# Scaling the first expert's outputs: GpSimd for groups 0 and 1, gated ScalarE for the others, in a linear attention and mixture-of-experts kernel

## The chip, the cores and the metric

One core of a Trainium2 chip runs the whole program. The metric is the device time of one execution in microseconds, the median of several runs. A core has TensorE (PE, matmuls into PSUM), VectorE (DVE), ScalarE (ACT), GpSimd (POOL, which here reads and writes SBUF only) and SyncE (SP, used here to issue DMAs). Each engine works through its own instruction queue in order; semaphores tie the queues together.

## The reference

The first half is linear attention over 8 batches and 8 heads (576 rows each, 64 wide); its output becomes `x` of 4608 rows by 512. The second half, where the change lies, is a mixture of 8 experts in which every row goes through every expert, weighted by a table `P` that a Sinkhorn iteration balances:

```python
logits = x @ w_gate
P = np.exp(logits - logits.max())
for _ in range(8):
    P /= P.sum(1, keepdims=True) + 1e-09
    P /= P.sum(0, keepdims=True) + 1e-09
    P *= N / E
out = np.zeros((N, D), dtype=np.float32)
for e in range(E):
    h = np.maximum(x @ w1[e], 0.0)
    ye = h @ w2[e]
    out += P[:, e:e + 1] * ye
```

`w1[e]` is 512 by 1024, `w2[e]` is 1024 by 512. The term of expert 0 is `P[:, 0:1] * y0`, and the sum over experts runs in an accumulator in SBUF.

## The kernel before

**Tiling.** The 4608 rows are nine groups g of 512 rows. `acc[g]` is the float32 accumulator of a group, four tiles `ts` of 128 rows by 512. Accumulators 0 to 4 live in SBUF from the start and serve as landing buffers for attention inputs at first; 5 to 8 are allocated when the attention's buffers are released (the event "late").

**Expert 0** (lines 749 to 804, 882 to 885) runs in ordinary matmuls, partly between the attention's steps. At that time P isn't known yet, so `down0` copies its result unscaled from PSUM into `acc[g]`: tiles with even `ts` on VectorE (L802), with odd `ts` on ScalarE (L795); `up0` has its relu on ScalarE (L760). Meanwhile `routing` computes P (its last step is L945 on VectorE).

**Experts 1 to 7** (lines 1284 to 1304) use a Strassen-like scheme with seven products in place of eight. For each expert, `sums_w` makes sums of weight blocks on VectorE (L986: first four for `w1`, then four for `w2`). For each group, `up7` makes 14 up products (names x1, y1, x2, w1, x3, x4, w2, each for two halves `fp`; a product is four matmuls of 256 columns, L1078). Its helpers empty the PSUM banks: `keep` copies a bank into a buffer U on ScalarE (L1106), `add` adds U and a bank into `hT` on VectorE (L1110), `relu` writes `hT` on ScalarE (L1115). A bank that `keep` has copied takes the next product on top (x1, x2, x3, x4 in one bank), so the next product waits for the copy. `down7` makes four sums S of `hT` blocks (L986) and seven down products of eight matmuls each, X1, Y1, Z1, X2, X3, Z2, X4. `read` adds P times a bank into an accumulator on VectorE (L1218). `read2` does it in two steps: ScalarE writes P times the bank into a buffer V (L1230, there are two V), and GpSimd adds V into the accumulator (L1233). The products go through `read2` for X1 and Y1 into block (0,0) and for Z1 and X3 into block (1,1), through `read` for the others.

**Order.** The down products of group g lie between the up products of group g+1, by

```python
ORDER = "X1 x10 w10 x11 X2 x20 y10 x21 Z1 y11 X3 w11 x30 x31 x40 x41 w20 Y1 w21 X4 Z2".split()
```

so Y1 comes near the end of the next group's slot. The first group of expert 1 has expert 0's last down matmuls ahead of it, and no down products of its own scheme between its up products.

**The planner.** The order in which instructions enter each engine's queue isn't the order of the text. `Plan.op` records each operation with its engine, a duration from a model (for instance `act(el)`: el/1200 + 0.09 us; `pool(el)`: el x 1.64e-3 + 0.17 us), the keys that it reads (`r`) and writes (`w`), and a running number. A read waits for the last writer of its key so far, a write for the last writer and all readers. `schedule` then takes, again and again, the operation that can start earliest by the model, at equal start the one with the lowest number. An operation marked `shared` (all of GpSimd's, and VectorE's sums L986 and some of the routing's) also waits until the one before it that was marked `shared` is done (`self.port`). The order so found is written into the queues; on the chip only the order and the semaphores remain.

**The scaling.** For expert 1, `down7` multiplies the accumulator of its group by column 0 of P, four operations of 128x512 on ScalarE (L1240). They need P, the unscaled result of expert 0 in `("acc", g, ts)` and, for accumulators 5 to 8, `akey(g)`, which is "late". They write `("acc", g, ts, j)` for both column halves j, and the reads of the down products (L1218, L1233) add on top of that. They have no other dependency: all 36 can start as soon as P and the tile are there. The operations of the group's S sums have lower numbers than its scaling, its down products and all later groups have higher ones.

Of the kernel before, what the change touches and what calls it, by code (L numbers as in the profile page):

```python
# [12 lines left out]
ALU = mybir.AluOpType  # L13
ACT = mybir.ActivationFunctionType
# [214 lines left out]
def kernel(  # L229
# [11 lines left out]
    nc = tc.nc  # L241
# [3 lines left out]
    N, DD = out.shape  # L245
# [24 lines left out]
    P = const.tile([128, NT, E], FP32, name="P")  # L270

    NA = 5
    acc = [accp.tile([128, 4, DD], FP32, name=f"acc{g}", tag=f"acc{g}") for g in range(NA)]
# [20 lines left out]
    def act(el, fn, r=(), w=()):  # L294
        plan.op("ACT", el / 1200.0 + 0.09, 0.22, fn, r, w)

    def dve(el, fn, r=(), w=(), shared=False):
        plan.op("DVE", el / 960.0 + 0.09, 0.22, fn, r, w, shared=shared)

    def pool(el, fn, r=(), w=()):  # L300
        plan.op("POOL", el * 1.64e-3 + 0.17, 0.25, fn, r, w, shared=True)
# [49 lines left out]
    def new(tag):  # L351
        return banks.new(int(tag[1])) if tag in ("P1", "P2") else R[tag].new()
# [426 lines left out]
    def akey(g):  # L779
        return ["late"] * (g >= NA) + ["P"] * (g >= 9)  # L780
# [31 lines left out]
    for i, (queue, eng) in enumerate((("ACT", nc.scalar), ("POOL", nc.gpsimd))):  # L812
        dma(queue, 1 << 15, 100, lambda i=i, eng=eng: eng.dma_start(
            out=wphi_f[64 * i:64 * i + 64, :], in_=w_phi), w=[f"wphi_f{i}"])
# [4 lines left out]
    for i in range(2):  # L819
        dve(64, lambda i=i: nc.vector.tensor_copy(  # L820
            out=wphi2[64 * i:64 * i + 64, i, :], in_=wphi_f[64 * i:64 * i + 64, :]),
# [4 lines left out]
    for h0 in (4, 6):  # L826
# [3 lines left out]
        out=wgate, in_=moe_w_gate.rearrange("(c p) e -> p c e", p=128)), w=["wgate"])  # L830
    for i in range(2):
        for x in range(2):
            dve(300, lambda i=i, x=x: nc.vector.memset(vrd[i][x], 0.0),
                w=[("vrd", i, x, h, *y) for h in range(2) for y in ((), (1,))])
# [147 lines left out]
    def sub(eng, el, out_, x, y, op, r, w):  # L982
        f = nc.vector if eng is dve else nc.gpsimd
        kw = {"shared": True} if eng is dve else {}
        eng(el * 0.6 if eng is dve else el * 1.04 + 128,
            lambda: f.tensor_tensor(out=out_(), in0=x(), in1=y(), op=op), r, w, **kw)  # L986
# [85 lines left out]
    def product(bank, lhs, rhs, nk, r, first, takes=(), wk=()):  # L1072


        for i in range(2):
            for k in range(nk):
                z = i == 0 and k == 0
                pe(256, lambda i=i, k=k, z=z: nc.tensor.matmul(  # L1078
                    bank()[:, 256 * i:256 * i + 256], lhsT=lhs(k, i), rhs=rhs(k),
                    start=first and z, stop=k == nk - 1, skip_group_check=True),  # L1080
                    r, [bank, *(wk if z else ())], takes if z else ())
# [72 lines left out]
    def acc_part(g, i, j):  # L1154
        return lambda: acc[g][:, 2 * i:2 * i + 2, 256 * j:256 * j + 256]
# [17 lines left out]
    def down7(e, g, hT, B7):  # L1173


        def a(i, j):
            return lambda: hT[j]()[:, :, 256 * i:256 * i + 256]

        def hk(i, j):
            return [(hT[j], fp, i) for fp in range(2)]  # L1180

        late, seen = akey(g), set()
        S = [new("S") for _ in range(4)]
        S01 = dve
        sub(dve, 1024, lambda: S[2](), a(0, 0), a(1, 0), ALU.subtract, hk(0, 0) + hk(1, 0),
            [S[2]])
        sub(S01, 1024, lambda: S[0](), a(1, 0), a(1, 1), ALU.add, hk(1, 0) + hk(1, 1), [S[0]])
        sub(S01, 1024, lambda: S[1](), lambda: S[0](), a(0, 0), ALU.subtract,
            [S[0]] + hk(0, 0), [S[1]])
        sub(dve, 1024, lambda: S[3](), a(0, 1), lambda: S[1](), ALU.subtract,  # L1190
            [S[1]] + hk(0, 1), [S[3]])

        def prod(bank, lhs, y, r, first, more=()):
            f, r2 = B7[y]
            product(bank, lambda k, i: lhs()[:, k, 128 * i:128 * i + 128],
                    lambda k: f()[:, k, :], 4, r + r2 + (["P"] if e else late) + list(more), first)

        def start(bank, i, j):

            out_ = acc_part(g, i, j)  # L1200
            w = [("acc", g, 2 * i + n, j) for n in range(2)]
            if (i, j) in seen:
                dve(500, lambda: nc.vector.tensor_tensor(
                    out=out_(), in0=bank().rearrange("p (a b) -> p a b", a=2), in1=out_(),
                    op=ALU.add), [bank] + late, w)
            else:
                act(512, lambda: nc.scalar.copy(
                    out=out_(), in_=bank().rearrange("p (a b) -> p a b", a=2)),
                    [bank] + late, w)
            seen.add((i, j))  # L1210

        def read(bank, i, j):

            if e == 0:
                return start(bank, i, j)
            for n in range(2):
                ts = 2 * i + n
                dve(330, lambda n=n, ts=ts: nc.vector.scalar_tensor_tensor(  # L1218
                    out=acc[g][:, ts, 256 * j:256 * j + 256],
                    in0=bank()[:, 256 * n:256 * n + 256], scalar=P[:, 4 * g + ts, e:e + 1],  # L1220
                    in1=acc[g][:, ts, 256 * j:256 * j + 256], op0=ALU.mult, op1=ALU.add),
                    [bank, "P"], [("acc", g, ts, j)])

        def read2(bank, i, j):

            if e == 0:
                return start(bank, i, j)
            u = new("V")
            for n in range(2):
                act(390, lambda n=n: nc.scalar.activation(  # L1230
                    out=u()[:, n, :], in_=bank()[:, 256 * n:256 * n + 256], func=ACT.Copy,
                    bias=0.0, scale=P[:, 4 * g + 2 * i + n, e:e + 1]), [bank, "P"], [(u, n)])
            pool(670, lambda: nc.gpsimd.tensor_tensor(  # L1233
                out=acc[g][:, 2 * i:2 * i + 2, 256 * j:256 * j + 256],
                in0=acc[g][:, 2 * i:2 * i + 2, 256 * j:256 * j + 256], in1=u(), op=ALU.add),
                [(u, 0), (u, 1)], [("acc", g, 2 * i + n, j) for n in range(2)])

        if e == 1 and g < 9:
            for ts in range(4):
                act(512, lambda ts=ts: nc.scalar.activation(  # L1240
                    out=acc[g][:, ts, :], in_=acc[g][:, ts, :], func=ACT.Copy, bias=0.0,
                    scale=P[:, 4 * g + ts, 0:1]), ["P", ("acc", g, ts)] + akey(g),
                    [("acc", g, ts, j) for j in range(2)])
        x, y, z = new("P1"), new("P1"), new("P1")

        def X1():
            prod(x, a(0, 0), "11", hk(0, 0), True, S[1:3])
            read2(x, 0, 0)

        def Y1():  # L1250
            prod(y, a(0, 1), "21", hk(0, 1), True)
            read2(y, 0, 0)

        def Z1():
            prod(z, lambda: S[0](), "t1", [S[0]], True, S[3:4])
            read2(z, 1, 1)

        def X2():
            prod(x, lambda: S[1](), "t2", [S[1]], False)
            read(x, 0, 1)  # L1260

        def X3():
            prod(x, lambda: S[2](), "t3", [S[2]], False)
            read2(x, 1, 1)

        def Z2():
            prod(z, lambda: S[3](), "22", [S[3]], False)
            read(z, 0, 1)

        def X4():  # L1270
            prod(x, a(1, 1), "t4", hk(1, 1), False)
            read(x, 1, 0)

        def stores():
            if e == E - 1:
                for ts in range(4):
                    store(g, ts)

        return {"out": stores, "X1": X1, "Y1": Y1, "Z1": Z1, "X2": X2, "X3": X3, "Z2": Z2, "X4": X4}
# [4 lines left out]
    for e in range(1, E):  # L1284
        w1, w2 = load_w(e, ["late"])
        if e == 1:
            for g in range(NG):
                sums_x(g)
        A7, B7 = sums_w(e, w1, w2)
        for g in (range(NG) if e < E - 1 else [8, *range(8)]):  # L1290
            X = load_x(g)
            hT = [new("hT") for _ in range(2)]
            un = up7(A7, g, X, hT, ["up0"])
            for n in ORDER:
                if len(n) == 3:
                    un[n[:2], int(n[2])]()
                elif dn is not None:
                    dn[n]()
            if dn is not None:
                dn["out"]()  # L1300
            if e == E - 1 and g == 7:
                down8(e, g, hT, w2)
            else:
                dn = down7(e, g, hT, B7)
# [31 lines left out]
```

## Time and profile before

| | |
|---|---|
| median of 3 runs | 1036.67 us (1035.63 to 1037.01) |
| the profiled execution | 1036.16 us |
| its span from first to last instruction | 1034.4 us |
| granted TensorE clock | 1.000 |
| TensorE busy (matmul) | 1013.8 us, 98% of the span |
| weight loads | 843.0 us, 81% |
| VectorE busy | 823.7 us, 80% |
| ScalarE busy | 710.9 us, 69% |
| GpSimd busy | 462.8 us, 45% |

In the page's 40 slices, the busy tenths show attention and expert 0 in the first ten slices and the experts after them:

```profile
PE   7899999999999999999999999999999999999998
PEld 5666666645788888888888888888888888888886
...
ACT  7999999837966666666666656666666566666653
POOL 5877675400243443434443444434444433334442
```

A digit is the busy share of a slice of 25.9 us in tenths; 9 is 90% or more. The span is that of the profiled execution, whose own time is 1.76 us longer. Matmuls are pipelined and overlap in the records, so the number of matmuls in a stretch says more than the busy time.

### The profile page before, as it was taken

The page shows a single profiled execution, that of the slowest core. Times are in us where ns is not written, and L with a number is a line of the kernel's source. Part 1 is how long each engine was busy: PE and PEld are TensorE (multiplying, and loading weights), DVE is VectorE, ACT ScalarE, POOL GpSimd, SP SyncE. Part 2 cuts the span into 40 slices and gives each one's busy share as a digit, 9 for nine tenths or more (in the row PEclk, how much of TensorE's full clock was granted, in tenths as well). Part 3 has the DMA queues.
Part 4 walks back from the last instruction along what each step waited for, and adds up shares of the span by engine and source line. Part 5 has one row for each costly group of instructions (what it writes and reads, how often), then busy time and mean ns, then how long its engine had stood idle before and what let it go on. Part 6 is the DMA issues. An engine that isn't in the chain of part 4 may idle for free.

```text
span 1034.4 us, 24481 instructions
## 1 busy us (share of the span) xinstructions
PE 1013.8 (98%) x9476; PEld 843.0 (81%) x9512; DVE 823.7 (80%) x1626; ACT 710.9 (69%) x1569; POOL 462.8 (45%) x534
## 2 busy tenths in 40 slices
PE   7899999999999999999999999999999999999998
PEld 5666666645788888888888888888888888888886
DVE  7999998987677788778777787788677877786775
ACT  7999999837966666666666656666666566666653
POOL 5877675400243443434443444434444433334442
PEclk9999999999999999999999999999999999999999
DMA  9998996085311161115211341134111611114333
GB/s 261 175 172 145 174 162 103 2 206 140 83 42 52 46 120 41 42 46 100 73 44 50 82 83 42 42 83 92 33 52 44 131 43 42 42 51 124 123 123 123
DMA packets 105237, 93.93 MB, mean 91 GB/s; under 512 B 45392, under 2 KB 80272, under 8 KB 105120
## 3 DMA queue, kind: packets, MB, share of 16 engines
q1 hardware_dynamic: 71360, 68.44, 24.3%
q0 software_dynamic: 33680, 23.90, 16.5%
q8 instruction: 74, 1.21, 0.5%
q14 instruction: 43, 0.35, 0.1%
q10 hardware_dynamic: 80, 0.03, 0.0%
HBM read 94.98 MB, written 14.16 MB: 106 GB/s over the span
## 4 chain that ended last, share of the span: by engine, by line
PE 92%; ACT 4%; DVE 3%; issue 1%; DMA 0%; DVEq 0%; POOLq 0%
PE P L1078 73%; PE P L468 17%; ACT acc L1240 2%; PE P L667 1%; DVE m L460 1%; ACT k L464 1%; PE P L706 1%; ACT q L464 0%; DMA wphi_f<-in_w_phi_dram 0%; DVE xb L687 0%; ACT U L1106 0%; DVE P L679 0%; PE P L672 0%; DVE S L986 0%; DVE m_r L460 0%
## 5 line engine op out<-in xcount | busy, mean ns | idle before, releaser
L1233 POOL TENSOR_TENSOR acc<-acc,V 128x512 f32<-128x512 f32 x248 | 316.1, 1281 | 440.5 <-ACT V L1230 437.6
L1110 DVE CUSTOM_DVE_ANT_0 hT<-P,U 128x512 bf16<-128x512 f32 x378 | 255.1, 687 | 105.9 <-ACT U L1106 56.7
L1106 ACT COPY U<-P 128x512 f32<-128x512 f32 x378 | 217.9, 590 | 139.0 <-PE P L1078 131.0
L1230 ACT ACTIVATE V<-P 128x256 f32<-128x256 f32 x496 | 205.6, 474 | 124.4 <-PE P L1078 119.2
L1218 DVE SCALAR_TENSOR_TENSOR acc<-P,acc 128x256 f32<-128x256 f32 x372 | 160.0, 478 | 73.7 <-PE P L1078 71.6
L1078 PEld LDWEIGHTS <-w 128*128 128x128 bf16 x2016 | 197.2, 98 | 25.2 <-issue 2.0
L1078 PEld LDWEIGHTS <-S 128*128 128x128 bf16 x1984 | 194.2, 98 | 22.4
L1078 PEld LDWEIGHTS <-T 128*128 128x128 bf16 x1512 | 147.9, 98 | 19.7 <-issue 2.5
L1078 PEld LDWEIGHTS <-hT 128*128 128x128 bf16 x1488 | 145.5, 98 | 17.1 <-DVE hT L1110 0.3
L1078 PE MATMUL P<-X,w 128*128 128x256 bf16 x1008 | 154.9, 273 | 0.4 <-ACT U L1106 0.4
L1078 PE MATMUL P<-xT,w 128*128 128x256 bf16 x1008 | 152.5, 273 | 0.9 <-ACT acc L795 0.5
L1078 PE MATMUL P<-X,T 128*128 128x256 bf16 x1008 | 148.6, 273 | 1.5 <-ACT U L1106 1.5
L1078 PE MATMUL P<-w,hT 128*128 128x256 bf16 x992 | 143.4, 273 | 0.0
L1078 PE MATMUL P<-T,S 128*128 128x256 bf16 x1056 | 136.3, 273 | 0.0
L1078 PE MATMUL P<-w,S 128*128 128x256 bf16 x928 | 126.5, 273 | 0.0
L460 DVE TENSOR_REDUCE m<-P 128x4 f32<-128x512 f32 x128 | 83.7, 679 | 3.4 <-PE P L468 2.1
L593 POOL TENSOR_TENSOR v<-v_m,em 128x512 bf16<-128x512 f32 x64 | 67.0, 1046 | 43.1 <-ACT em L464 39.0
L986 DVE TENSOR_TENSOR S<-hT 128x1024 bf16<-128x1024 bf16 x124 | 83.4, 709 | 0.3 <-ACT hT L1115 0.3
L1115 ACT ACTIVATE hT<-P 128x512 bf16<-128x512 f32 x126 | 74.2, 604 | 12.4 <-PE P L1078 11.9
L468 PE MATMUL P<-w,hT 128*128 128x512 bf16 x303 | 77.1, 379 | 0.9 <-DVE m L460 0.2
L1078 PE MATMUL P<-xT,T 128*128 128x256 bf16 x504 | 76.0, 273 | 0.3
L468 PE MATMUL P<-xT,w 128*128 128x512 bf16 x271 | 71.4, 379 | 1.0 <-ACT q L464 0.3
(95 smaller groups left out, 1096.5 us busy)
## 6 DMA issues: line engine op xcount, KB each, us to landing
X<-xd SPq DMA_DIRECT2D x126, 256.0 KB, 2.6
w<-in_moe_w_dram POOLq DMA_DIRECT2D x14, 1024.0 KB, 10.1
v_m<-in_v_dram SPq DMA_DIRECT2D x14, 512.0 KB, 5.2
out_dram<-acc SPq DMA_DIRECT2D x14, 512.0 KB, 2.7
xd<-S SPq DMA_DIRECT2D x18, 256.0 KB, 2.4
qk<-in_k_dram POOLq DMA_DIRECT2D x12, 256.0 KB, 5.5
qk<-in_q_dram POOLq DMA_DIRECT2D x12, 256.0 KB, 6.5
w<-in_moe_w_dram POOLq DMA_DIRECT2D x8, 256.0 KB, 7.7
```

What stands on the lines that cost most here:

```text
L460: dve(el, lambda: nc.vector.tensor_reduce(out=dst(), in_=src(), axis=AX.X, op=ALU.max, apply_absolute_value=True), r, w)
L468: nc.tensor.matmul(out_, lhsT=lhsT, rhs=rhs, start=start, stop=stop)
L593: pool(512, lambda y=y, em=em: nc.gpsimd.tensor_tensor(out=s["v"][y]()[:, :, 0:D], in0=t["v"]()[:, h0:h0 + 2].rearrange("p a (b c) -> p (a ...
L986: lambda: f.tensor_tensor(out=out_(), in0=x(), in1=y(), op=op), r, w, **kw)
L1078: pe(256, lambda i=i, k=k, z=z: nc.tensor.matmul(bank()[:, 256 * i:256 * i + 256], lhsT=lhs(k, i), rhs=rhs(k), start=first and z, stop=k = ...
L1106: act(512, lambda: nc.scalar.copy(out=u[fp][n]().rearrange("p a b -> p (a b)"), in_=x[fp]()), [x[fp]], [u[fp][n]])
L1110: dve(500, lambda: nc.vector._custom_dve(ADD_SAT, out=out_(fp, i, j), in0=bank[fp]().rearrange("p (a b) -> p a b", a=2), in1=u[fp][n](), s ...
L1115: act(512, lambda: nc.scalar.activation(out=out_(fp, i, j), in_=x[fp]().rearrange("p (a b) -> p a b", a=2), func=ACT.Relu, bias=0.0, scale ...
L1218: dve(330, lambda n=n, ts=ts: nc.vector.scalar_tensor_tensor(out=acc[g][:, ts, 256 * j:256 * j + 256], in0=bank()[:, 256 * n:256 * n + 256 ...
L1230: act(390, lambda n=n: nc.scalar.activation(out=u()[:, n, :], in_=bank()[:, 256 * n:256 * n + 256], func=ACT.Copy, bias=0.0, scale=P[:, 4 ...
L1233: pool(670, lambda: nc.gpsimd.tensor_tensor(out=acc[g][:, 2 * i:2 * i + 2, 256 * j:256 * j + 256], in0=acc[g][:, 2 * i:2 * i + 2, 256 * j: ...
L1240: act(512, lambda ts=ts: nc.scalar.activation(out=acc[g][:, ts, :], in_=acc[g][:, ts, :], func=ACT.Copy, bias=0.0, scale=P[:, 4 * g + ts, ...
```

## The change

In `down7`, for expert 1: groups 0 and 1 are scaled on GpSimd by a `tensor_tensor` multiplication with the column of P broadcast along the row, the others on ScalarE as before. From group 2 on, the scaling also reads the key `("acc", g - 2, 0, 0)`. When `down7(1, g)` is called, the down products of group g-1 are recorded and so are those of group g-2; the last writer of that key is then GpSimd's add of Y1 of group g-2. So the four scalings of group g wait for that add. Groups 0 and 1 have no such key. The planner's model gives a GpSimd scaling 670 x 1.64e-3 + 0.17 = 1.27 us and marks it `shared`; the ScalarE one keeps 512/1200 + 0.09 = 0.52 us.

```diff
         if e == 1 and g < 9:
             for ts in range(4):
-                act(512, lambda ts=ts: nc.scalar.activation(
-                    out=acc[g][:, ts, :], in_=acc[g][:, ts, :], func=ACT.Copy, bias=0.0,
-                    scale=P[:, 4 * g + ts, 0:1]), ["P", ("acc", g, ts)] + akey(g),
-                    [("acc", g, ts, j) for j in range(2)])
+                r = ["P", ("acc", g, ts)] + akey(g) + ([("acc", g - 2, 0, 0)] if g >= 2 else [])
+                w = [("acc", g, ts, j) for j in range(2)]
+                if g < 2:
+                    pool(670, lambda ts=ts: nc.gpsimd.tensor_tensor(
+                        out=acc[g][:, ts, :], in0=acc[g][:, ts, :],
+                        in1=P[:, 4 * g + ts, 0:1].to_broadcast([128, DD]), op=ALU.mult), r, w)
+                else:
+                    act(512, lambda ts=ts: nc.scalar.activation(
+                        out=acc[g][:, ts, :], in_=acc[g][:, ts, :], func=ACT.Copy, bias=0.0,
+                        scale=P[:, 4 * g + ts, 0:1]), r, w)
```

## The prediction

> **What bounds the kernel now.** I read the windows view first, cut where the stages change (its columns: busy microseconds and instructions of TensorE, its weight loads, VectorE, ScalarE, GpSimd; then clock, DMA share, GB/s).
>
> ```profile
> core 0: us, PE busy (x) PEld busy (x) DVE busy (x) ACT busy (x) POOL busy (x), PEclk, DMA share, GB/s
> 245.10:254.10 9.00, 8.91 (x42) 3.99 (x41) 5.79 (x11) 9.00 (x17) 0.75 (x1) 1.00 0.78 146
> 254.10:268.60 14.50, 11.50 (x94) 8.88 (x93) 9.93 (x16) 14.50 (x27) 0.89 (x1) 1.00 0.60 110
> 268.60:280.80 12.20, 12.20 (x112) 10.88 (x112) 8.65 (x16) 12.00 (x25) 5.08 (x4) 1.00 0.16 44
> 280.80:354.00 73.20, 73.20 (x673) 65.62 (x671) 53.84 (x97) 45.98 (x97) 30.32 (x24) 1.00 0.15 44
> 354.00:1000.00 646.00, 645.92 (x5918) 578.77 (x5916) 498.90 (x889) 405.02 (x846) 278.89 (x222) 1.00 0.28 69
> ```
>
> From 268.6 on TensorE is the floor: 112 matmuls in 12.2 us is 0.109 us each, and 5918 in 646 us is the same 0.109. Nothing on another engine can be won there. Between 245 and 268.6 it is otherwise: ScalarE is busy for the whole of both rows, and TensorE starts 94 matmuls where 14.5 us hold 133.
>
> The chain of waits from 236 to 300 us says who holds TensorE up (start, length, piece):
>
> ```profile
> 243.45 1.33 ACT acc L1240 x2
> ...
> 248.07 3.67 ACT acc L1240 x6
> 251.74 0.48 ACT acc L795
> 252.22 2.43 ACT acc L1240 x4
> ...
> 263.30 1.38 ACT acc L1240 x3
> 264.68 0.31 issue
> 264.99 1.98 ACT acc L1240 x3
> 266.96 0.47 ACT U L1106
> ...
> 268.58 31.44 PE P L1078 x286
> ```
>
> L1240 is the operation that the change moves. The reader is to see that it stands in ScalarE's queue ahead of work that TensorE waits for (L795 and L1106 empty PSUM banks), and that after 268.58 the chain is TensorE alone. The timeline shows the largest single case:
>
> ```profile
> 263.15 3.81 ACT L1240 ACTIVATE acc<-acc,P 128x512 f32<-128x512 f32 x6
> ...
> 266.82 0.61 ACT L1106 COPY U<-P 128x512 f32<-128x512 f32 x1
> ...
> 267.48 0.60 PE L1078 MATMUL P<-X,T 128*128 128x256 bf16 x4 [1.33 <-ACT U L1106]
> ```
>
> Six scalings in a row take 3.81 us, the copy of U behind them starts only at 266.82, and TensorE stands for 1.33 us.
>
> **What the stall is worth.** In 254.1 to 268.6 the 94 matmuls need 94 x 0.109 = 10.3 us, so 14.5 - 10.3 = 4.2 us are lost. In the stretch before, the matmuls are 512 columns wide:
>
> ```profile
> 243.44 1.89 PE L468 MATMUL P<-xT,w 128*128 128x512 bf16 x8
> 245.17 8.34 PE L468 MATMUL P<-w,hT 128*128 128x512 bf16 x36
> 253.35 0.27 PE L1078 MATMUL P<-xT,w 128*128 128x256 bf16 x1
> ```
>
> Eight of them take 245.17 - 243.44 = 1.73 us, 0.216 each; 36 need 7.78, and 253.35 - 245.17 = 8.18, so 0.4 is lost. The ceiling of the gain is 4.2 + 0.4 = 4.6 us.
>
> The Trainium skill (page "Trainium Kernel Development and Optimization", section "Performance Expectations") says that matmul busy time is a bad measure, since matmuls are pipelined, and that weight loads are a good one. The trace agrees: matmul busy of 11.50 in 14.50 would put the loss in that row at 3.0 us, while 93 weight loads against 112 in 12.2 us put it at 4.4. By busy time the sum below would end 1.2 us higher.
>
> **The change, part by part.** *Removed from ScalarE's early queue: all 36 scalings.*
>
> ```profile
> L1240 ACT ACTIVATE acc<-acc,P x36: 706/740/885, 243.4 to 278.3; 128x512 f32<-128x512 f32 x36
> ```
>
> Back to back they cost 3.67 / 6 = 0.61 us of ScalarE, 22 us in all, now packed into 243 to 279. Groups 0 and 1 (8 of them) leave the engine; the other 28 cannot start before GpSimd's last add into accumulator (0,0) of the group two before. The first such adds come here:
>
> ```profile
> 254.57 0.89 POOL L362 DMA_DIRECT2D w<-in_moe_w_dram  x1 [8.18 <-PE P L468]
> 269.35 1.27 POOL L1233 TENSOR_TENSOR acc<-acc,V 128x512 f32<-128x512 f32 x1 [13.90 <-ACT V L1230]
> 272.27 1.27 POOL L1233 TENSOR_TENSOR acc<-acc,V 128x512 f32<-128x512 f32 x1 [1.65 <-ACT V L1230]
> ```
>
> So no scaling is left on ScalarE in the stretch that loses time: up to 4.6 us.
>
> *What stays of the stall.* Expert 1's first group has no down products to lie between its up products. A chain step is a product of 4 matmuls (0.44), their tail (0.27 - 0.11 = 0.16), one copy of U and the hand-over:
>
> ```profile
> L1106 ACT COPY U<-P 128x512 f32<-128x512 f32 x37 | 21.5, 587 | 16.4 <-PE P L1078 16.1
> ```
>
> (groups of 280.8 to 354, where it runs undisturbed; the add on VectorE from the page's groups)
>
> ```profile
> L1110 DVE CUSTOM_DVE_ANT_0 hT<-P,U 128x512 bf16<-128x512 f32 x378 | 255.1, 687 | 105.9 <-ACT U L1106 56.7
> ```
>
> That is about 1.25 us a step (0.05 for the hand-over is my estimate, from U's end at 267.43 to TensorE's start at 267.48). Laid along the order of the 14 products (x1, w1, x2, y1, x3, x4, w2 for two halves), with 0.69 for the add ahead of w2, the first group ends about 6.7 us after its start where its products need 14 x 0.436 = 6.1: 0.6 lost. The down products then wait for the last add and the S sums on VectorE (0.69 each, the L986 rows below), which group 1's first products cover in part: I take 0.6 more. So 1.2 stay, an estimate; the ends are 0 and 4.2, the whole loss of that stretch.
>
> *Added on GpSimd: 8 multiplications of 128x512 with a broadcast scalar.* The trace has none in f32 out; the nearest rows are
>
> ```profile
> L1233 POOL TENSOR_TENSOR acc<-acc,V 128x512 f32<-128x512 f32 x248 | 316.1, 1281 | 440.5 <-ACT V L1230 437.6
> L593 POOL TENSOR_TENSOR v<-v_m,em 128x512 bf16<-128x512 f32 x64 | 67.0, 1046 | 43.1 <-ACT em L464 39.0
> ```
>
> 1.05 (a broadcast, bf16 out) to 1.28 us; I take 1.28, the row with f32 out: 10.2 us. They can start at 243.4, when P is there (L945 in the timeline below), and GpSimd is otherwise empty until 269.35 except for two issues of DMA (0.75 and 0.89): done near 255. The first add that needs them would come at 269.35 - 4.6 = 264.7, so 9 us cover them, price 0. Without that cover each microsecond would hold the adds, then the two buffers of V, then ScalarE. The load of expert 2's weights, issued on the same queue, may go out some microseconds later; its weights are used nine groups of 12.2 us later.
>
> *The port.* The planner never lets a GpSimd operation run beside a VectorE sum of two SBUF inputs (`shared`). VectorE's timeline shows these sums, with P ahead of them and one later place:
>
> ```profile
> 242.96 0.45 DVE L945 TENSOR_TENSOR P<-T,c_bc 128x288 f32<-128x288 f32 x1
> ...
> 244.60 1.29 DVE L986 TENSOR_TENSOR T<-w 128x1024 bf16<-128x1024 bf16 x2
> ...
> 249.43 1.28 DVE L986 TENSOR_TENSOR T<-w,T 128x1024 bf16<-128x1024 bf16 x2
> ...
> 398.09 1.26 POOL L1233 TENSOR_TENSOR acc<-acc,V 128x512 f32<-128x512 f32 x1 [0.53 <-ACT V L1230]
> ...
> 398.15 1.74 DVE L986 TENSOR_TENSOR S<-hT 128x1024 bf16<-128x1024 bf16 x1
> ```
>
> The row at 398.15 shows what a meeting costs on the chip: a sum that takes 0.69 takes 1.74 beside a GpSimd add. Expert 1's products need its first four sums (x, 244.6 to 247.1) by 253.35, 6 us later. Sums come before scalings at equal start, by their earlier number, so scalings slip in while VectorE does one of its three copies out of PSUM (groups of 243.4 to 268.6):
>
> ```profile
> L802 DVE COPY acc<-P 128x512 f32<-128x512 f32 x3 | 2.1, 689 | 2.1 <-PE P L468 2.1
> ```
>
> Each such case delays the sums by 1.28 - 0.69 = 0.6, 1.8 in all, within the 6. Price 0. If all eight went first, the four sums would end at 243.4 + 10.2 + 0.4 + 4 x 0.69 = 256.8 (0.4 for one sum of half the length that is left from the sums of x), 3.4 late: that is the other end.
>
> The Trainium skill (page "SBUF — State Buffer", section "Who interferes with whom") says that such a VectorE instruction and a GpSimd one take the same port, whoever starts first for its whole length, and the other blocks. The row at 398.15 agrees. By the rule with GpSimd first, the sum would give back 3.4; it is a rival below.
>
> *Added to ScalarE in expert 1's slots: 4 gated scalings per group, seven groups.* A group is 12.2 us; ScalarE is busy 45.98 / 6 = 7.7 of it, so 4.5 are idle and 4 x 0.61 = 2.4 fit. That density has been on this chip already, and more:
>
> ```profile
> 270.00:280.00 10.00, 5.22 (x7) 1.00 0.20 54
> ```
>
> Seven scalings (L1240 alone) stood in 10 us there, with TensorE at its floor (112 in 12.2). What is new is the wait: the planner puts the first scaling at the moment at which it believes GpSimd's add to end, and where the add is late, the copies of U and the V scalings queue behind it, and TensorE behind those. Ends: 0, and the 1.33 us seen above in each of seven groups, 9.3. ScalarE's idle 4.5 speaks for the low end; I take 0.3 in all.
>
> *The rest.* The planner orders everything after the change anew. Of 765 us nothing can be won; the one place where it lost anything is
>
> ```profile
> 397.52 0.02 issue
> 397.55 0.04 DVE hT L1110
> 397.58 0.57 issue
> 398.15 1.74 DVE S L986
> ```
>
> I take 0; the other end is 0.57 at each of six changes of expert, 3.4.
>
> **The sum.** -4.6 + 1.2 + 0 + 0 + 0.3 + 0 = -3.1 us. The profiled execution took 1036.16 (span 1034.4 and 1.76 around it), so 1033.1 for its like; the median of the runs, 1036.67, lies 0.5 above it, so I say 1033.6.
>
> **The rivals.** (1) *The first group is bound by its own chain*, not by ScalarE: 3 us of the stall stay instead of 1.2, time 1035.4. For it: VectorE waits for U, and no down products lie between. Against: the pieces of the chain before 268.58 are scalings, 1.3 to 3.7 us at a time. Chance 0.10.
> (2) *Slower: the gate blocks ScalarE's queue.* The scaling waits at the head of the queue for GpSimd's 1.27-us add, seven times, and each time a copy of U is 1.33 late: -4.6 + 1.2 + 9.3 = +5.9, 1042.6. It decides from (3.4 + 2.1) / 7 = 0.8 us a group. For it: the planner places it at the earliest moment, with no reserve. Against: 4.5 idle us a group, and seven ungated scalings in 10 us cost nothing. Chance 0.12.
> (3) *The port*: the scalings go ahead of the sums, 3.4 late, nothing is won: -3.1 + 3.4, 1037.0. Against: the order of numbers above. Chance 0.05.
> (4) *The new order limps at changes of expert*, +3.4: 1037.0. For: VectorE is the second busiest engine. Against: six changes lose almost nothing now. Chance 0.05, of which 0.02 for worse than +2.
> That the change doesn't clear ScalarE can be excluded: a gated scaling cannot run before group 0's adds.
>
> **How the numbers follow.** A measurement of this kernel tells 0.2%, 2.1 us, from no change: 1034.6 to 1038.7 is the same. The forecast has 0.68 and lies below 1034.6, with its own range 1032.1 (all 4.6 won) to 1034.6. Same: 0.10 + 0.05 + 0.03 = 0.18. Slower: 0.12 + 0.02 = 0.14. The range goes from 1031.6 (0.5 below the best, the distance of profile and median) to 1037.4, which takes in rivals 1 and 3 and leaves out the slower ones.
>
> **What would show it.** Right: between 245 and 268 no L1240 on ScalarE, ScalarE with idle time, the matmuls up to group 1 about 3 us earlier, eight GpSimd multiplications of 1.05 to 1.28 us done well ahead of its first add; four scalings in each later group of expert 1 and TensorE at 112 matmuls in 12.2 us there. Wrong: TensorE waiting for U behind a scaling that itself waits for GpSimd (rival 2); the first up products later than 253.4 (rival 3); gaps of the same length with ScalarE idle (rival 1); matmuls below 0.109 a piece after 354 (rival 4).

## The result, and the profile after

The changed kernel takes 1039.63 us (median of 9 runs, 1038.82 to 1041.12), the kernel before 1037.01 (9 runs, 1035.63 to 1038.63): a ratio of 1.0029, 95% interval 1.0019 to 1.0038. It is slower by 2.6 us where 3.1 us less were forecast.

The chain of waits of the changed kernel from 236 us on (start, length, piece), to set beside the chain of before in the prediction:

```profile
245.67 1.21 DVE T L986 x2
246.88 8.51 DVE w L986 x2
255.38 0.60 DVE T L986
255.99 0.61 DVE acc L802
256.60 0.04 issue
256.64 4.33 PE P L468 x13
...
261.73 7.33 PE P L1078 x67
269.06 0.02 issue
269.08 0.59 ACT U L1106
269.67 0.04 issue
269.71 756.48 PE P L1078 x6928
```

The scalings on ScalarE, which filled the chain before, are gone from it. In their place stand two VectorE sums of 8.51 us together, where two such sums take 1.28, and behind them a copy out of PSUM (L802). After 269.71 the chain is TensorE alone, as it was before after 268.58. The timeline shows who holds the sum:

```profile
244.25 1.15 POOL L1243 TENSOR_TENSOR acc<-acc,P 128x512 f32<-128x512 f32 x1 [35.75 <-DVE P L945]
246.38 0.81 POOL L362 DMA_DIRECT2D w<-in_moe_w_dram  x1 [0.99 <-PE P L468]
247.21 7.02 POOL L1243 TENSOR_TENSOR acc<-acc,P 128x512 f32<-128x512 f32 x7
...
246.80 8.59 DVE L986 TENSOR_TENSOR w<-w 128x1024 bf16<-128x1024 bf16 x2
...
256.64 4.33 PE L468 MATMUL P<-w,hT 128*128 128x512 bf16 x13 [5.38 <-DVE acc L802]
```

Seven scalings run one behind the other on GpSimd from 247.21 to 254.23, 1.0 us each. The second of the two sums starts at 247.4 and ends at 255.39, 1.16 us after the last scaling. The copy of expert 0's group 8 stands two places behind it in VectorE's queue; TensorE needs that bank and stands for 5.38 us.

The windows of the changed kernel, with the columns of the prediction's first fence:

```profile
251.10:256.64 5.54, 0.16 (x1) 0.00 (x0) 5.54 (x5) 0.60 (x1) 3.13 (x4) 0.94 0.54 102
256.64:260.81 4.17, 4.17 (x14) 1.58 (x14) 2.03 (x4) 0.00 (x0) 0.00 (x0) 0.66 0.00 0
260.81:269.71 8.90, 8.67 (x76) 7.35 (x75) 5.29 (x9) 5.63 (x10) 0.95 (x1) 1.00 0.71 115
269.71:281.91 12.20, 12.20 (x112) 10.93 (x112) 10.43 (x20) 9.66 (x20) 5.03 (x4) 1.00 0.34 91
281.91:355.10 73.19, 73.19 (x673) 65.57 (x672) 55.80 (x100) 56.99 (x118) 30.59 (x24) 1.00 0.15 44
355.10:1000.00 644.90, 644.90 (x5910) 578.03 (x5908) 496.30 (x888) 407.00 (x849) 278.10 (x220) 1.00 0.28 69
```

In the first row TensorE does nothing: 5.5 us lost. In the second, 13 matmuls of 512 columns (the row's fourteenth starts as it ends) take 4.17 us where 13 x 0.216 = 2.8 is their floor: 1.4 lost, at a granted clock of 0.66. Microsecond by microsecond (TensorE alone: busy and instructions, clock, DMA share, GB/s) the clock is at half for three and full again after the fourth:

```profile
256.00:257.00 1.00, 0.36 (x1) 0.51 0.00 0
257.00:258.00 1.00, 1.00 (x4) 0.50 0.00 0
258.00:259.00 1.00, 1.00 (x4) 0.50 0.00 0
259.00:260.00 1.00, 1.00 (x5) 0.78 0.00 0
260.00:261.00 1.00, 1.00 (x7) 1.00 0.00 0
```

In the third row expert 1's first products lose 0.4. That makes 7.3 us lost in the opening against 4.6 before, 2.7 more; the medians differ by 2.6. From 269.71 on, TensorE is at 112 matmuls in 12.2 us, in the groups with the moved scalings too (fifth row, ScalarE 56.99 of 73.19 against 45.98 before).

### The profile page after: what moved, and what is told of

Its sections match the earlier page's. It is cut to its first block, busy times and chain, and to the rows that moved or that the text cites. A ratio compares the mean times of both kernels' runs of the same rounds, so it can differ in the third digit from the quotient of the medians.

```text
span 1037.5 us, 24533 instructions
## 1 busy us (share of the span) xinstructions
PE 1014.4 (98%) x9512; PEld 842.4 (81%) x9512; DVE 828.3 (80%) x1626; ACT 706.1 (68%) x1561; POOL 473.0 (46%) x542
## 4 chain that ended last, share of the span: by engine, by line
PE 94%; DVE 3%; ACT 2%; issue 0%; DMA 0%; DVEq 0%
PE P L1078 74%; PE P L468 18%; PE P L667 1%; DVE w L986 1%; ACT q L464 1%; ACT k L464 1%; DVE m L460 1%; PE P L706 1%; PE P L545 0%; DVE xb L687 0%; PE P L672 0%; DMA acc<-in_k_dram 0%; DVE P L679 0%; DVE m_r L460 0%; DVE T L986 0%
## 5 line engine op out<-in xcount | busy, mean ns | idle before, releaser
L593 POOL TENSOR_TENSOR v<-v_m,em 128x512 bf16<-128x512 f32 x64 | 67.0, 1046 | 44.0 <-ACT em L464 39.9
L468 PE MATMUL P<-w,hT 128*128 128x512 bf16 x320 | 81.0, 384 | 5.6 <-DVE acc L802 5.4
L468 PE MATMUL P<-xT,w 128*128 128x512 bf16 x288 | 74.7, 379 | 0.3 <-ACT q L464 0.3
```

Of the source, the lines that this page charges most:

```text
L468: nc.tensor.matmul(out_, lhsT=lhsT, rhs=rhs, start=start, stop=stop)
L593: pool(512, lambda y=y, em=em: nc.gpsimd.tensor_tensor(out=s["v"][y]()[:, :, 0:D], in0=t["v"]()[:, h0:h0 + 2].rearrange("p a (b c) -> p (a ...
```

## The experiments

Theory A: GpSimd's run of scalings holds the VectorE sum, the copy behind the sum is late, TensorE stands, and the stand costs it the clock. The rivals are that the gate (the key of the group two before) or the new order costs the time, or that GpSimd's scalings cost it in another way. All times are medians, beside runs of the kernel before on the same chip (1037.08 for e1 to e4, 1037.02 for e5 to e8); brackets hold the 95% interval of the ratio to it. Each diff is against the changed kernel.

**e1: no scaling on GpSimd.**

```diff
-                if g < 2:
+                if False:
```

> All scalings on ScalarE: groups 0 and 1 ungated, the others gated as in the changed kernel. Theory A (in the changed kernel, GpSimd's seven scalings in a row hold a VectorE sum of two SBUF inputs for 8 us, the copy out of PSUM behind it is late, TensorE stands 5.4 us and then runs at half clock): without GpSimd's scalings no sum of expert 1 takes over 0.7 us, TensorE's gap of 5.4 us is gone, and since the gate has cleared ScalarE, the time is about 1033.5, 3.5 below the kernel before. Theory B (the gate itself, or the new order that it brings, costs the time later): 1037 or more, with TensorE waiting for U or below its floor in expert 1's groups.

1034.55 us, ratio 0.9976 [0.9968, 0.9985]. The gap is gone, so the gate and the clearing of ScalarE are a gain by themselves: 2.5 us. That is 1 less than expected, and the trace says where. In the windows (weight loads alone) from 270 us on, ten microseconds hold 92 or 93 loads, in one case 90, and in one late stretch 84, about 0.9 us lost. The chain into it holds a sum S of 1.74 us at 347.96 and a weight sum of 1.67 us at 355.03, each beside an add on GpSimd:

```profile
350.00:360.00 10.00, 8.14 (x84) 1.00 0.14 35
360.00:370.00 10.00, 8.97 (x92) 1.00 0.77 150
```

**e2: GpSimd's part without the gate.**

```diff
-                r = ["P", ("acc", g, ts)] + akey(g) + ([("acc", g - 2, 0, 0)] if g >= 2 else [])
+                r = ["P", ("acc", g, ts)] + akey(g)
```

> Groups 0 and 1 on GpSimd as in the changed kernel, the other 28 scalings on ScalarE without the gate. Theory A: the sum is held for about 8 us again and TensorE stands about 5 us; the 28 early scalings run on ScalarE in the meantime. 1039 to 1041. Theory B (the gate costs the time): without the gate 1037 or less.

1042.64 us, ratio 1.0055 [1.0041, 1.0069], 1.6 above the upper end of what was expected. Two sums take 8.58 us and TensorE's gap is 5.38 again. This time the 13 matmuls behind it take 5.47 us (256.09 to 261.56), and the early scalings on ScalarE make TensorE wait for U for 1.6 us more. So the gate isn't what costs: taking it away adds 3.

**e3: GpSimd's scalings read the key of the last weight sum.**

```diff
                 if g < 2:
+                    r = r + B7["t4"][1]
```

> As the changed kernel, but GpSimd's scalings also wait for the last of expert 1's eight weight sums. Theory A: no weight sum takes over 0.7 us, no gap of TensorE before expert 1, the scalings run from about 252 to 260 and are still ahead of GpSimd's first add: about 1033.5. If GpSimd's scalings cost in another way (their length, the adds behind them, the DMA issue), the loss stays: 1037 to 1040.

1041.26 us, ratio 1.0044 [1.0032, 1.0057], above both ranges that were expected. The timeline tells why.

```profile
246.87 8.01 POOL L1244 TENSOR_TENSOR acc<-acc,P 128x512 f32<-128x512 f32 x8
...
246.27 9.76 DVE L986 TENSOR_TENSOR w<-w 128x1024 bf16<-128x1024 bf16 x2
...
257.89 5.32 PE L468 MATMUL P<-w,hT 128*128 128x512 bf16 x13 [6.91 <-DVE acc L802]
```

The scalings start at 246.87, before the sums that the new key names. A key orders operations in the planner. On the chip these scalings did not wait for that sum, whose tile they neither read nor overwrite. With the DMA issue no longer between the first scaling and the others, eight run in a row, the hold grows by one scaling (9.16 us for the held sum, 7.99 in the changed kernel) and the gap to 6.91.

**e4: the copies of expert 0's last group on ScalarE.**

```diff
-            if ts % 2:
+            if ts % 2 or g == 8:
                 act(512, lambda i=i, ts=ts: nc.scalar.activation(
```

> As the changed kernel, but the copies of expert 0's group 8 out of PSUM are all on ScalarE, so none of them stands behind the held sum on VectorE. Theory A, with the copy as the link from the sum to TensorE: a sum still takes about 8 us, the gap of 5.4 us inside expert 0's last matmuls is gone, and TensorE waits instead at expert 1's first product for the held sums, 2 to 3 us, too short for the half clock: 1035 to 1037. If TensorE's gap has another cause than that copy, it stays at 5 us: 1039 to 1040.

1033.52 us, ratio 0.9971 [0.9959, 0.9982], below what was expected. The hold is there in full and costs next to nothing:

```profile
247.43 8.59 DVE L986 TENSOR_TENSOR w<-w 128x1024 bf16<-128x1024 bf16 x2
...
254.53 0.27 PE L1078 MATMUL P<-xT,w 128*128 128x256 bf16 x1
...
259.08 0.60 PE L1078 MATMUL P<-X,w 128*128 128x256 bf16 x4 [0.68 <-DVE hT L1110]
```

So the link from the sum to TensorE is the copy that stands behind it. The 2 to 3 us at expert 1's first product did not come either: products start at 254.53, before the last four sums have run. In the code the first product lists sums as keys that it doesn't multiply by; those, too, are order and no wait.

**e5: half the scalings.** Group 0 on GpSimd, group 1 on ScalarE without a gate.

```diff
-                if g < 2:
+                if g < 1:
```

> Only group 0 is scaled on GpSimd (four scalings); group 1 is scaled on ScalarE without a gate. Theory A (each scaling holds VectorE's sum for its 1.0 us, and a run of them for the whole run): three scalings in a row hold the sum for about 3.5 us instead of 8, TensorE's gap before the copy shrinks from 5.4 to about 1.4 us, too short for the half clock: 1034 to 1035. If the hold doesn't follow from the number of scalings (one meeting is enough): gap and time as in the changed kernel, 1039 to 1040.

1036.72 us, ratio 0.9997 [0.9989, 1.0006]. The hold and the gap are near what was expected (3.5 and 1.4 us):

```profile
248.05 3.04 POOL L1243 TENSOR_TENSOR acc<-acc,P 128x512 f32<-128x512 f32 x3
...
247.63 4.61 DVE L986 TENSOR_TENSOR w<-w 128x1024 bf16<-128x1024 bf16 x2
...
253.50 2.96 PE L468 MATMUL P<-w,hT 128*128 128x512 bf16 x13 [1.41 <-DVE acc L802]
256.30 0.27 PE L1078 MATMUL P<-xT,w 128*128 128x256 bf16 x1
```

Three in a row hold the sum to 1.15 us after the last of them, 4.01 us in all, the gap is 1.41, and the 13 matmuls take 2.80 us, their floor. The time is 1.7 over the range: this order has TensorE waiting for hT and V for 1.4 us in expert 1's first down products, and for hT for 0.8 more in a late stretch of 84 weight loads, as in e1.

**e6: no scaling at all.**

```diff
-        if e == 1 and g < 9:
+        if e == 1 and g < 0:
```

> No scaling of expert 0's outputs at all (that part of the computation is left out). It shows what the stretch costs when neither ScalarE nor GpSimd has the 36 scalings: the predicted ceiling was 4.6 us less what expert 1's first group loses to its own chain, taken as 1.2: 1033 to 1034. If the chain costs as much as the whole stall of before, 1036 to 1037; if next to nothing, 1032 to 1033.

1032.68 us, ratio 0.9965 [0.9953, 0.9978], a little below the 1033 to 1034 expected. This kernel leaves out the weighting of expert 0's term; it gives the floor of the edit, 4.3 below before.

**e7: memsets in place of the scalings.**

```diff
-                    pool(670, lambda ts=ts: nc.gpsimd.tensor_tensor(
-                        out=acc[g][:, ts, :], in0=acc[g][:, ts, :],
-                        in1=P[:, 4 * g + ts, 0:1].to_broadcast([128, DD]), op=ALU.mult), r, w)
+                    pool(670, lambda ts=ts: nc.gpsimd.memset(acc[g][:, ts, :], 0.0), r, w)
```

> Each of GpSimd's eight scalings is replaced by a memset of the same accumulator tile, which reads nothing from SBUF (expert 0's term is left out in groups 0 and 1); the order on VectorE and TensorE is that of the changed kernel. Theory A with the read path as the shared thing: no weight sum takes over 0.8 us, the copy is in time, no gap: 1033 to 1034. If any GpSimd instruction on SBUF holds the sum, or if the order itself is at fault: a sum takes some microseconds and the gap stays, 1037 to 1040.

1032.64 us, ratio 0.9959 [0.9946, 0.9973]. This kernel leaves out expert 0's term in groups 0 and 1. The timeline, and the group of the sums that were held (durations in ns, least, median, most):

```profile
247.38 3.35 POOL L1243 MEMSET acc<- 128x512 f32 x7
...
246.81 1.28 DVE L986 TENSOR_TENSOR w<-w 128x1024 bf16<-128x1024 bf16 x2
```

```profile
L986 DVE TENSOR_TENSOR w<-w x2: 683/684/684, 246.8 to 247.4; 128x1024 bf16<-128x1024 bf16 x2
```

Seven GpSimd instructions in a row, in the same place and the same order, and the sums beside them take 0.68. What holds the sum is therefore neither the order nor GpSimd being busy or writing. The scalings read SBUF and the memsets don't, so the runs point to the reading. The memsets are also shorter (0.48 against 1.0), but no sum is longer by even one of them.

**e8: a wait that the chip keeps.** VectorE copies P's column for groups 0 and 1 into a small tile right after the last sum, and GpSimd multiplies by that.

```diff
+        if e == 1 and g == 0:
+            dve(8, lambda: nc.vector.tensor_copy(out=Pc, in_=P[:, 0:8, 0]),
+                ["P"] + B7["t4"][1], ["Pc"])
...
                 if g < 2:
+                    r = r + ["Pc"]
...
-                        in1=P[:, 4 * g + ts, 0:1].to_broadcast([128, DD]), op=ALU.mult), r, w)
+                        in1=Pc[:, 4 * g + ts:4 * g + ts + 1].to_broadcast([128, DD]), op=ALU.mult), r, w)
```

> As the changed kernel, but GpSimd multiplies by a copy of P's column that VectorE makes right after the last weight sum of expert 1, so that the chip itself holds the scalings back by a semaphore (the key of e3 ordered them only in the planner). Theory A: no weight sum over 0.7 us, no gap, the scalings run from about 252 to 260: 1033 to 1034. If GpSimd's scalings cost something beside the hold of those sums (a later meeting with VectorE, adds that come late), 1035 or more.

1032.95 us (1032.64 to 1033.15), ratio 0.9962 [0.9949, 0.9974]: faster than both kernels, by 4.1 and 6.7 us, and within 0.3 of the kernel that scales nothing. Line numbers are one higher here up to the new lines.

```profile
251.36 0.17 DVE L1240 COPY Pc<-P 128x8 f32<-128x8 f32 x1
...
251.61 8.03 POOL L1248 TENSOR_TENSOR acc<-acc,Pc 128x512 f32<-128x512 f32 x8 [4.50 <-DVE Pc L1240]
...
267.75 2.61 POOL L1234 TENSOR_TENSOR acc<-acc,V 128x512 f32<-128x512 f32 x2 [7.21 <-ACT V L1231]
```

The same eight scalings, seven of which began at 247.21 in the changed kernel, run in a row from 251.61, beside VectorE instructions that read PSUM, and are done 8 us ahead of the first add. A further cost of theirs is not seen: e6 is 0.3 us faster, and its order differs too. Expert 1's eight sums stay under 0.7 us, as expected. A later weight sum takes 1.74 us at 270.75, beside an add on GpSimd, and TensorE then waits 0.64 us for hT.

## Why the prediction was wrong

**What bounded the kernel before: right.** The scalings in ScalarE's queue cost TensorE 4.6 us by the count of matmuls; without any scaling the kernel is 4.3 faster (e6). What stays in expert 1's first group was put at 1.2; it is 0.4 in the changed kernel, and about 1.4 in the order of e6.

**The scalings on GpSimd: right, and shorter.** 1.28 was taken, 1.0 each came, near the broadcast row of L593. They were to be done near 255 and are done at 254.23.

**The port: the step that failed.** It was put at price 0, because "the planner never lets a GpSimd operation run beside a VectorE sum of two SBUF inputs" and scalings slip in singly while VectorE copies. The planner did plan it so. These are its own starts for GpSimd's scalings in the changed kernel, by its model, in us:

```
246.78  252.11  254.84  256.84  258.11  259.38  260.65  261.92
```

But that is an order within each queue, and nothing on the chip holds GpSimd back between them: the seven after the first were planned over 11 us, the last five in a row only once the sums were through, and they ran in 7 us, beside the sums. The second part of the failure is the size of a meeting. The row at 398.15 showed a sum held by one add, 1.05 us, and each meeting was priced as one such instruction. A run holds the sum until the run ends: 3 scalings gave 4.01 us, 7 gave 7.99, 8 gave 9.16, against 0.68 (e5, the changed kernel, e3). The third part is what stands behind the held sum. The other end and rival 3 priced only the sums as late for expert 1's first product (3.4 us). That product did not wait (e4); the copy out of PSUM, two places behind in VectorE's queue, did, and with it TensorE. The price was 5.5 us of standing and 1.4 at the lower clock. So rival 3 had the right cause, but the wrong path to TensorE and too small a price, and the range, which ends at 1037.4, lies below the 1039.63 measured.

One reading under that price was wrong as well. The prediction takes the sums from 244.6 to 247.1 for the first four that expert 1's products need, done 6 us ahead. By their forms each of the four rows of weight sums of before (244.60, 245.80, 247.01 and 249.43) holds one sum of `w1` and one of `w2`. So the last of `w1` stands in the row at 249.43, and the cover was about 3 us.

The rule on the port that the prediction cites from the Trainium skill (page "SBUF — State Buffer", section "Who interferes with whom") pointed the right way and was set aside for the planner's order. The same section says that a VectorE instruction with two SBUF inputs contends with a GpSimd one that reads SBUF and not with one that only writes it; e7 agrees, 0.68 us beside the memsets.

**The clock: not thought of.** The page "TensorE: Matmul & The Clock Gate", section "Part 1: The HAM clock gate (the "warmup" mystery)", of the Trainium skill says that an idle window of about 3.4 us halves TensorE's clock. The rows agree: 0.50 after a gap of 5.38 us, and none of it after 1.41 (e5).

**The gate: harmless, for another reason than given.** The text above the prediction and rival 2 take the key of the group two before as a wait of ScalarE. e3 shows that such a key only places an operation in the queue, and the changed kernel's own timeline shows it for the gate:

```profile
278.38 2.50 POOL L1233 TENSOR_TENSOR acc<-acc,V 128x512 f32<-128x512 f32 x2 [1.08 <-ACT V L1230]
...
279.11 1.94 ACT L1247 ACTIVATE acc<-acc,P 128x512 f32<-128x512 f32 x3
```

Group 2's first gated scaling starts at 279.11. The last two of group 0's four adds, Y1's among them, run from 278.38 to 280.88, so the add that the gate names isn't done. The wait on which rival 2 rests isn't there on the chip. TensorE kept its floor through expert 1 (112 in 12.2 us, with ScalarE at 9.5 of 12.2), so the 0.3 reserved for it was not spent.

**The rest: right in the changed kernel.** 5910 matmuls in 644.9 us are 0.109 each. Rival 4 showed itself in e1 and e5, with about 0.9 us in one stretch, and with less in e2 (546 weight loads from 360 to 420 us, 550 in the changed kernel).

With the hold taken away, the changed kernel comes to 1032.95 (e8), 4.1 below before. So 3.1 was a little low for the gain of what the edit means to do, and the miss is the hold and the stand of TensorE that follows from it.

## What to carry to other kernels

A planner's resource rule is worth only what the semaphores enforce: an engine that has no data to wait for runs its queue as early as it can, so look at what a run of its instructions meets then, and not at the planned times. When one instruction may be held, price the whole run of the other engine, and then name what stands behind the held instruction in its queue and who waits for that. If an order must hold on the chip, give it a real dependency; here one copy of eight columns of P turned a loss of 2.6 us into a gain of 4.1.

## What the runs showed of the hardware that was not expected

A VectorE sum that waited for GpSimd was not let in between two scalings on GpSimd that followed one another without a gap: one of 0.68 us ended 1.15 to 1.16 us after the end of runs of 3, 7 and 8. Memsets of GpSimd on the same tiles held it not at all. And a stand of TensorE costs more than its length once it is long: after 1.41 us the next 13 matmuls took 2.80 us, after 5.38 us 4.17 and 5.47 (the changed kernel and e2), after 6.91 us 5.16 (257.89 to 263.05 in e3). Why the same gap of 5.38 us cost 1.4 us in one kernel and 2.7 in the other is not shown.
